# Two heads in one state product: an attention scan ahead of two feed-forward nets on one core

## The chip, the cores and the metric

The kernel runs on one core of a Trainium2 chip. The time is the device time of one execution in microseconds (us). Three executions of the kernel before took 524.62, 525.79 and 525.80 us; their median, 525.79 us, is the time before. One execution was recorded by the hardware profiler, and all rows below come from it.

The engines have short names: PE is TensorE (PEld its weight loads), DVE is VectorE, ACT is ScalarE, POOL is GpSimd, SP is the engine that issues transfers. Each runs its own instructions in order and waits on the others by semaphores. PSUM is the memory into which PE writes its sums; SBUF is the memory that all other operands live in.

## The reference, cut to what matters

Four batches of 768 rows, 8 heads, head size 32 (D), state size 16 (N). A chunked linear attention makes x, and two feed-forward nets follow, the second without a nonlinearity:

```python
for c in range(nc):                      # chunks of 32 in the reference
    L = exp(cum_i - cum_j) * causal
    y = (C B^T * L) x  +  (C state) * exp(cum)
    state = decay_full * state + sum_j B_j x_j * decay_from_j
x = y.reshape(3072, 256)
h = x @ w_in                             # 256 -> 2048
x = where(h > 0, h, exp(min(h, 0)) - 1) @ w_out
h = (x @ w1) * (x @ w2) @ w3             # 1024 wide
out = h @ w_out2                         # 256
```

## The kernel before, in words

**Tiling.** Time runs in 24 chunks of 128 columns (`k`; each is two sub-blocks `s` of 64), four to a tile of 512 columns (`t`, six tiles). A tile of `x` has its 256 features on 2 times 128 partitions. Every operand of the large products is kept as a high and a low float32r word (`mm3`, L381 to 384: three products of 128x128 by 128x512 for one exact one). A cast on ACT makes the high word, a subtraction (`take_lo`, L161) the low one.

**The scan.** `unit_u` (L658) makes, for two chunks, C times B (`cb_products`, L511) and the new part of the states (`u_products`, L548). A state tile has 128 rows: four groups of 32, each two heads of 16 states; its 64 columns are the 32 values of either head. So half of a group's block, the rows of one head under the values of the other, holds numbers that belong to no head. `decayed` (L526) and `states` (L559) follow on DVE. `unit_y` (L670) runs `y_products` (L582): for each chunk 16 products of x with the decayed C times B (L590), and then, for each chunk, sub-block, head of the pair (`g`) and group (`q`), one product of the 32 by 32 columns of that head with C (L598); C is laid out with zeros for the other head's 16 rows (`cd`, L530, made on POOL). `turned` (L544) moves the groups of odd chunks by one, so that group `q` of an even and of an odd chunk stand on different rows. `made_x` (L683) casts the result to xT and subtracts.

**The first net.** `unit_a` (L706) makes h of 256 features for one tile: 12 products of 512 columns; then `elu` (L713): exp and relu on ACT, a maximum on DVE (L722), the high word on ACT (L727), the low word on DVE (L729). `unit_b` (L737) multiplies by w_out: again 12 products. `half_a` (L701) makes only the first 256 columns of tile 0 for feature block `n`, into `early_h`; `unit_a` then makes the other half, if that `half_a` has run already.

**Weights.** They arrive as 64-bit words; each piece (L192) is shifted (`k`, DVE), scaled (`j`, ACT), joined (`K`, DVE), cast (`H`, ACT) and its low word taken (`I`).

**The second net** (`by_product`, `last_product`) runs from about 344 us on, on sums of its operands (one level of a seven-product scheme); its low words (`,`) and its sums (`}`, `>`, `{`) are on DVE, the operand sums (`*`) and half of the gates (`<`) on POOL.

**What sets the order.** The string `ORDER` (L37): each letter runs the next waiting step of its kind, and `in_order` (L646) fixes that each engine runs its instructions in the order in which the letters issue them. Nothing else plans. A step that waits holds back all that stands behind it on its engine.

Of the kernel before, what the change touches and what calls it, by code (L numbers as in the profile page):

```python
# [14 lines left out]
Q = 128  # L15
SUB = 2
# [21 lines left out]
094AAlU7AlC5Al5UCJCD566l8jCNk5K8JkHND6IjDQjND6KkHNkKQzzYNYzIvzjYNYjkaKjk!HaKXjkxIkNjKarkKMjsHMxKbIrNKxsXrLaHkBjLN8j8vsxX  # L38
BHKuWkPIrbDHMKjkIMKbWINsRXaWHLCNjLBbxCDrCttBjNsCakhVkiyxIrKbXkzsWzMHYYuhKNIaHiXIDbxDNrttjsyVaKzXzkHYYhNVaIxijMrkKbMsHxPL
raINhLjsaxijNhRbxXrLCCiaMSBSBrsBCbshxirLahKBiaxksHrIkbjsxCNKrKuHksbhItDVahtDjijykxirbMKHsMzbzhYPiNYuhKbXHtDtDjkyLaBzIzYY  # L40
INiaxKrXLHbHIsxNkhIRa1jBrMiaCxNCsrKwXxshkNribfsjCXjKHuFhMIatjDHNLIakxCDSiSr1bKxtLNrwsjskykfHFKhIaMzzHKjINibBkMBxYKYbhNri
PsuhbXjDtiXwtkDLykfhFRaHXHIziBNbxIYjLrwzBsNYKukHMfIbjFDMKtHNaDILXCkwxBLCNhtrKajsfjKhiaxiHrkIbFKHxINsrbhskyhSwPjzzYYMKiaH
XSIijMfBakxCFNHCrIaXxsrRwxsrsbfjKkFLahBiuLxbrtBDCHDItbshiKyhHbzXIzYi1CuhYMaDDXttwixMrLBafNLsbBxCFrCkNjsyhazijYkbKxzKr3Y%
&su&h=bitbhtD&D=y=S&Saz=YNziaxYrsaNh3xibxkrrbsshiahjijKbxkK%&ra&s^=hb=&ix&=ar=Nsax1rh3aNxirksb3jxKs@jakK%&=a@#&h3rib&s@&
=x=b=h#Nri^ahs^xia@N#rk#jxsbrKsaSkjSKh%b@i&=xb^h&@=#ahi&ribx#s3r1xsb&=h3^@iar=hbix/srsbh/i|ch_bmi/|#b_/G|e]_gncS[Em({|G}
)]_e>gn<c[*Em(.{G})],<e.>En,g.{*c[,(m)S}*g.1>e.,*G[<3nc,.d*](,mE.}G.{d.,<e],)ng>E,.c{[*dm,(G*.}d.<e]*,d$.d,$),ng>.d+*.(,
[dc,$E}.d@{em,<@d#nG#d*3]g@+)[#^(>E}*c@{e.<dn^dm+d@#G.,)]#*g$>E@(.#^[c{3.d}*m),.e.,G<ng>](,@^E[}c,dm,e.#g.,Gd,*]d{E+n*).
<d.{d[*,(>d)+*c}d+m<e.,2gn>3G[+(]c.}dm,E.3,d.,G.,d,*g{e<dn*)+.(]+2*d.}E.>[d{.c,<2em,).Gn*>g],d.,d.,c[E,md,*({G}*.d<]).e*
>$d,.g*n,c[d.+($,2dm,E.}G.,d]{e$,<)@+gn#d[*(>@E}.*c{e<dn#d.,^)m+d@.g#^@G>.d,@*d+@d#](^.,E[c{*dm}).#G<.>e@#dng]#c[,Em,({G
}g],).,e,*En>d[d+*.d{c<*dm,).+(.*G>.g}.d],<[e+En+2c.,dm{(d}d,G,e]<)$,g.+*dn>2[d,c*.+(.d}*.d,2mE,G*.e{d,n<).,d.>g](,[c,E}  # L50
m*d{e*dnG.)],(.>*d$}E.<g.,d.{[c,<$d+me$,2).g,d+[d>nG.d.d.+c],(mE}d,e{G,nd+]),g<(>.d$[d.Ed{}),<d>,d..,d,dd+++++
"""
HALF = 4
VECTOR_LO = 16
PIECES = [(("w_in", "w_out")[k == "o"], "iioiooiiiiooiooo"[:n].count(k)) for n, k in enumerate("iioiooiiiiooiooo")] + [("wo2", m) for m in range(4)] + [("w3", m) for m in range(16)] + [
# [36 lines left out]
XCOLS = (("x", DM), ("bn", NH * N), ("bt", 2 * R), ("cz", 2 * 2 * R), ("cp", SUB * 2 * R))  # L92
# [3 lines left out]
def kernel(  # L96
# [42 lines left out]
    side = const.tile([P, 2], F32, name="side")  # L139
    sel = act.tile([P, 2, 2, TT], F32R, tag="g", name="sel")[:SUB * CPT, 0, 0].rearrange("p (k s i) -> p k s i", k=CPT, s=SUB)  # L140
    begun = const.tile([P, CPT * SUB, R], F32, tag="begun", name="begun")

    def constants():

        V.memset(side, 0.0)
        A.activation(side, side, AF.Exp)

        G.memset(eye2, 1.0)
        G.affine_select(out=eye2, in_=eye2, compare_op=ALU.is_equal, fill=0.0, base=0,
                        pattern=[[-R, SUB], [-1, R]], channel_multiplier=1)  # L150
        n = SUB * CPT
        A.copy(sel, eye2[:n, 0, :n].rearrange("p (k s o) -> p k s o", k=CPT, o=1).to_broadcast([n, CPT, SUB, R]))
        V.tensor_tensor(out=eye2[:, 0], in0=eye2[:, 0], in1=eye2[:, 1], op=ALU.add)
        V.tensor_copy(eye, eye2[:, 0:1].to_broadcast([P, NH, R]))
        G.memset(begun, 0.0)

# [35 lines left out]
    class Piece:  # L192


        def __init__(self, name, src, room, dst):
            self.name, self.src, self.room, self.dst = name, src, room, dst
            self.lo, self.word, self.parts, self.half = G, None, None, 0

# [232 lines left out]
    def at_load(k):  # L431
        c = ck[k]
        all_ = att.tile([P, XC], F32, tag="xbc", name=f"xbc{k}", bufs=4)
# [9 lines left out]
        c["cp"] = cols_["cp"].rearrange("p (s f) -> p s f", s=SUB)  # L443
# [99 lines left out]

    def turned(k, p):  # L544

        return (p + k % 2) % 4

    def u_products(k, u):  # L548


        c = ck[k]
        for p in range(4):
            for s in halves(k):
                rows = slice(R * s, R * s + R)
                to = turned(k, p)
                T.matmul(u[32 * to:32 * to + 32, s], c["bd"][rows, 2 * p:2 * p + 2].rearrange("p h n -> p (h n)"),
                         c["x"][rows, 64 * p:64 * p + 64], start=True, stop=True, skip_group_check=True)

    def states(k, u):  # L559
# [4 lines left out]
        for s in halves(k):  # L564
            V.scalar_tensor_tensor(out=new[:, s], in0=state[k, s], scalar=pr_of(k)[:, s, R - 1:R], in1=u[:, s],
                                   op0=ALU.mult, op1=ALU.add)
            state[(k, 1) if s == 0 else (k + CPT, 0)] = new[:, s]

    def first_states(k, u):
# [3 lines left out]
        state[k, 1], state[k + CPT, 0] = new[:, 0], new[:, 1]  # L573
        later("8", next_state, k)

    def next_state(k):

        kept = att.tile([P, 2 * D], F32, tag="kept", name=f"kept{k}", bufs=1)
        G.tensor_tensor(out=kept, in0=state[k, 1], in1=ck[k]["pr"][:, 1, R - 1:R].to_broadcast([P, 2 * D]), op=ALU.mult)
        G.tensor_tensor(out=state[k + CPT, 0], in0=state[k + CPT, 0], in1=kept, op=ALU.add)  # L580

    def y_products(*chunks):  # L582
        for k, both in chunks:
            c = ck[k]
            for g in range(2):
                for s in range(SUB):
                    rows = slice(R * s, R * s + R)
                    for q in range(4):
                        h = 2 * q + g
                        T.matmul(both[32 * q:32 * q + 32, s, g], c["x"][rows, D * h:D * h + D], c["L"][rows, h],  # L590
                                 start=g == 0, stop=(k, s) not in state, skip_group_check=True)
        for g in range(2):
            for s in range(SUB):
                for k, both in chunks:
                    for q in range(4) if (k, s) in state else ():
                        at = turned(k, q)
                        rows = slice(32 * at, 32 * at + 32)
                        T.matmul(both[32 * q:32 * q + 32, s, g], state[k, s][rows, D * g:D * g + D], ck[k]["cd"][rows, s, g],  # L598
                                 start=False, stop=True, skip_group_check=True)

    def x_room(k):
        t, s0 = k // CPT, (k % CPT) * Q
        if k % CPT == 0:
            xT[t] = [act.tile([P, 2, TT], F32R, tag=f"xx{p}", name=f"xT{p}{t}", bufs=3) for p in ("h", "l")]
        return [v[:, :, s0:s0 + Q].rearrange("p g (s i) -> p s g i", s=SUB) for v in xT[t]]

    def by_head(y):
        return y.rearrange("p s (g i) -> p s g i", g=2)

    def parts_of(room):  # L610

        cb, u, both = (room[:, :, a:b] for a, b in ((0, 4 * R), (4 * R, 4 * R + 2 * D), (4 * R + 2 * D, 6 * R + 2 * D)))
        return cb, u, by_head(both)
# [3 lines left out]
    def first_room_of(k):  # L617
# [3 lines left out]
                first_rooms[2 + half][:, :, R * (k % 2):R * (k % 2) + R],  # L621
                first_rooms[2 + k % 2][:, :, 2 * R * (1 + half):2 * R * (2 + half)])

    def first_cb(*ks):
        for k in ks:
            cb, u, y = first_room_of(k)
            ck[k]["room"] = u, by_head(y)
# [3 lines left out]
    def first_u(*ks):  # L631
        for k in ks:
            u_products(k, ck[k]["room"][0])
        for k in ks:
            later("6", first_states, k, ck[k]["room"][0])

    def first_y(*ks):
        y_products(*((k, ck[k]["room"][1]) for k in ks))
        for k in ks:
            later("z", made_x, k, ck[k]["room"][1], A)  # L640
# [29 lines left out]
    def unit_y(k):  # L670

        two = [(j, by_head(banks(f"y{j}")[:, :, :2 * R])) for j in (k, k + 1)]
        y_products(*two)
        for j, both in two:
            later("z", made_x, j, both, A if j < 2 * CPT else V)
# [7 lines left out]
    def made_x(k, both, hi_eng):  # L683
        hi, lo = x_room(k)
# [28 lines left out]
    def elu(t, n, h):  # L713
# [9 lines left out]
        if not plain:  # L723
# [4 lines left out]
            yield "i"  # L728
            take_lo(V, lo, e, hi)  # L729
# [279 lines left out]
    for n, p in enumerate(queue):  # L1009
        p.lo = V if 0 < n < VECTOR_LO else G  # L1010

# [97 lines left out]
```

## Time and profile before

| | us |
|---|---|
| three executions | 524.62, 525.79, 525.80 |
| the profiled execution, its own time | 524.71 |
| its span, first to last instruction | 523.0 |
| PE busy | 508.8 (97%) |
| DVE, ACT, POOL busy | 428.8 (82%), 323.6 (62%), 204.4 (39%) |
| moved | 52.66 MB in 28177 packets |

A row of grouped instructions reads: line, engine, operation, output from inputs, shape, count, then busy time and mean duration in ns of one, then the idle time of the engine ahead of them and what ended it. A recorded matmul lasts longer than its share of PE's time, since matmuls overlap: the distance from start to start is the cost. A float32 product has two records, a float32r product one.

### The profile page before, as it was taken

The numbers are of one execution on the slowest core, as the hardware profiler recorded it, in microseconds if no ns is written. First come the engines' busy times: TensorE is split into PE (matmuls) and PEld (weight loads), VectorE is DVE, ScalarE is ACT, GpSimd is POOL, SyncE is SP. The second block draws the span as 40 slices with busy tenths as digits, with TensorE's granted clock in tenths as the row PEclk, the third lists the DMA queues.
The fourth block names the chain that finished last, engine by engine and source line by source line (L and its number), as shares of the span: only waits on it lengthen the run. The fifth ranks groups of instructions, "written<-read, shape, count | busy, mean of one in ns | idle before, by whom it ended". The sixth has DMA issues, their size and how long they took to land.

```text
span 523.0 us, 10654 instructions
## 1 busy us (share of the span) xinstructions
PE 508.8 (97%) x4330; PEld 411.2 (79%) x4330; DVE 428.8 (82%) x589; ACT 323.6 (62%) x482; POOL 204.4 (39%) x184
## 2 busy tenths in 40 slices
PE   5799999999999999999999999999989999999996
PEld 3675788778888888878788888888777888888885
DVE  6888989879897996867766797869999989988845
ACT  2585587655754385535476787747766577765650
POOL 3223004205430544122203333967477465755401
PEclk9999999999999999999999999999999999999999
DMA  8993473147555635053202321001000110001002
GB/s 297 348 277 132 134 207 126 41 143 235 170 158 150 222 108 174 1 160 104 69 35 77 106 80 47 35 0 61 0 22 21 61 41 20 1 20 41 21 1 80
DMA packets 28177, 52.66 MB, mean 101 GB/s; under 512 B 2304, under 2 KB 10880, under 8 KB 28128
## 3 DMA queue, kind: packets, MB, share of 16 engines
q1 hardware_dynamic: 27984, 51.85, 30.4%
q8 instruction: 34, 0.56, 0.4%
q14 instruction: 15, 0.12, 0.1%
q10 hardware_dynamic: 144, 0.13, 0.1%
HBM read 45.58 MB, written 6.39 MB: 99 GB/s over the span
## 4 chain that ended last, share of the span: by engine, by line
PE 91%; DVE 6%; issue 1%; DMA 0%; ACT 0%; DVEq 0%
PE acc L382 9%; PE acc L384 9%; PE h L382 9%; PE acc L383 9%; PE h L383 9%; PE h L384 9%; PE p L382 4%; PE p L384 3%; PE p L383 3%; PE acc L745 3%; PE p_d L382 2%; PE p_d L384 2%; PE p_d L383 2%; PE p_E L382 2%; PE p_E L383 2%; PE p_E L384 2%
## 5 line engine op out<-in xcount | busy, mean ns | idle before, releaser
L715 ACT ACTIVATE e<-h 128x1024 f32<-128x1024 f32 x48 | 49.2, 1025 | 58.0 <-PE h L384 55.5
L382 PE MATMUL h<-xTh,w_in 128*128 128x512 f32 (+1 forms) x200 | 80.0, 400 | 0.8 <-ACT xTh L685 0.8
L383 PE MATMUL h<-xTl,w_in 128*128 128x512 f32 (+1 forms) x200 | 77.7, 389 | 0.0
L384 PE MATMUL h<-xTh,w_in 128*128 128x512 f32 (+1 forms) x200 | 77.5, 388 | 0.0
L162 DVE TENSOR_TENSOR g<-e,g 128x1024 fp32r<-128x1024 f32 x44 | 60.1, 1370 | 15.5 <-ACT g L727 15.4
L382 PE MATMUL acc<-g,w_out 128*128 128x512 f32 x176 | 69.6, 396 | 0.0
L722 DVE SCALAR_TENSOR_TENSOR e<-e,h 128x1024 f32<-128x1024 f32 x44 | 53.3, 1214 | 19.7 <-ACT e L717 19.6
L384 PE MATMUL acc<-g,w_out 128*128 128x512 f32 x176 | 68.6, 390 | 0.0
L383 PE MATMUL acc<-g,w_out 128*128 128x512 f32 x176 | 68.5, 389 | 0.0
L727 ACT CAST g<-e 128x1024 fp32r<-128x1024 f32 x44 | 46.2, 1049 | 30.0 <-PE acc L384 26.5
L717 ACT ACTIVATE e<-e 128x1024 f32<-128x1024 f32 x48 | 50.7, 1059 | 0.8
L382 PEld LDWEIGHTS h<-xTh,w_in 128*128 128x128 f32 x200 | 38.6, 193 | 9.4 <-issue 1.8
L383 PEld LDWEIGHTS h<-xTl,w_in 128*128 128x128 f32 x200 | 38.5, 193 | 7.8 <-issue 0.7
L384 PEld LDWEIGHTS h<-xTh,w_in 128*128 128x128 f32 x200 | 38.6, 193 | 7.6
L162 POOL TENSOR_TENSOR w<-raw_wc,w 128x512 fp32r<-128x512 f32 x16 | 23.9, 1502 | 51.5 <-ACT w L236 48.6
L536 POOL TENSOR_TENSOR xbc<-xbc,pr 128x256 f32<-128x256 f32 (+1 forms) x24 | 22.9, 965 | 50.9 <-DMA L<-a_cut 30.7
L382 PEld LDWEIGHTS acc<-g,w_out 128*128 128x128 f32 x176 | 33.0, 188 | 7.4
L384 PEld LDWEIGHTS acc<-g,w_out 128*128 128x128 f32 x176 | 33.0, 188 | 7.0
L383 PEld LDWEIGHTS acc<-g,w_out 128*128 128x128 f32 x176 | 33.1, 188 | 6.6
L504 POOL TENSOR_TENSOR xbc<-xbc,L 128x128 f32<-128x128 f32 x24 | 15.1, 634 | 58.1 <-DVE L L498 37.7
L899 POOL TENSOR_TENSOR room_l<-room_l,room_o 128x512 f32<-128x512 f32 x12 | 19.8, 1647 | 32.8 <-DVE room_o L896 19.1
L498 DVE TENSOR_TENSOR_SCAN L<-L,eye 128x512 f32<-128x512 f32 x20 | 27.3, 1368 | 2.0 <-DMA L<-a_cut 2.0
(427 smaller groups left out, 1278.2 us busy)
## 6 DMA issues: line engine op xcount, KB each, us to landing
xbc<-in_xc SPq DMA_DIRECT2D x24, 512.0 KB, 6.3
raw_wc<-in_w3t SPq DMA_DIRECT2D x16, 512.0 KB, 4.3
L<-a_cut SPq DMA_DIRECT2D x40, 128.0 KB, 4.8
raw_wi<-in_w_in SPq DMA_DIRECT2D x8, 512.0 KB, 8.6
raw_wo<-in_w_out SPq DMA_DIRECT2D x8, 512.0 KB, 6.4
x_dram<-x SPq DMA_DIRECT2D x6, 512.0 KB, 4.9
room_s<-x_dram SPq DMA_DIRECT2D x12, 256.0 KB, 4.3
out_t<-out SPq DMA_DIRECT2D x11, 256.0 KB, 2.0
```

The costliest lines, as they stand in the source:

```text
L162: eng.tensor_tensor(out=lo, in0=raw, in1=hi.bitcast(F32), op=ALU.subtract)
L382: T.matmul(out, wlo, xhi, start=first, stop=False, **kw)
L383: T.matmul(out, whi, xlo, start=False, stop=False, **kw)
L384: T.matmul(out, whi, xhi, start=False, stop=last, **kw)
L498: V.tensor_tensor_scan(out=flat, data0=wide, data1=eye.rearrange("p h s -> p (h s)"), initial=0.0, op0=ALU.mult, op1=ALU.add)
L536: G.tensor_tensor(out=c["cd"][:, n:], in0=c["cd"][:, n:], in1=c["pr"].rearrange("p s (o i) -> p s o i", o=1)[:, n:].to_broadcast([P, SUB - ...
L715: A.activation(e, h, AF.Exp)
L717: A.activation(e, e, AF.Relu, scale=-1.0, bias=1.0)
L722: V.scalar_tensor_tensor(out=gt[t, n] if plain else e, in0=e, scalar=-1.0, in1=h, op0=ALU.mult, op1=ALU.max)
L727: A.copy(hi, e)
L745: T.matmul(acc, word_of(n)[:, j, es], g[:, j], start=m == 0, stop=False)
L899: GATE[m % 2].tensor_tensor(out=s["two"], in0=s["two"], in1=s["u2"], op=ALU.mult)
```

## The change

State tiles are set to zero outside each head's own block, on POOL, by one multiplication with a mask (`own_heads`, letter `?`), 24 times. C is kept without its zeros, so `cd` multiplies half as many elements, and a chunk's transfer has 448 KB in place of 512 KB. One product takes 32 rows by all 64 columns of a group and so serves two heads. Outputs now go by four heads and two chunks to a PSUM tile, instead of by one chunk. `turned` is gone.

Beside it: 13 of the 44 low words of the elu (`T`) are taken on POOL; 21 of 44 weight shifts run on ACT; xT casts of chunks 8 to 15 run on ACT. The order of the first weight pieces is another (five of w_in first), and the whole `ORDER` string is another. In the string of before the second `v` (`half_a` of block 1) stands behind the third `a` that follows `a` of block 1; in the new one ahead of `a` of block 1. The new string starts with all four `A`, and moves DVE's `7` behind three scans (`l`).

```diff
-094AAlU7AlC5Al5UCJCD566l8jCNk5K8JkHND6IjDQjND6KkHNkKQzzYNYzIvzjYNYjk
+094AAlAl5Al5U7UJD6lk?C6j?!DNCkKC5jD5QHN8JKzIzY66NYHk?jD8kNK?jCI8QkNvK8zzY
...
+SCALAR_Z = 4
+POOL_LO = "001000100101000000010100101100001101000110000000"
+SCALAR_LOW = "11011000000110010000100011111001011110011100"
...
+        G.memset(head, 1.0)
...
+        V.tensor_reduce(out=own, in_=head.rearrange("p (b g) -> p g b", g=2), op=ALU.add, axis=AX.X)
...
         def shifted(self):
-            V.tensor_scalar(self.low, self.low, 29, None, op0=ALU.logical_shift_right)
+            if self.scalar_low:
+                A.activation(self.low, self.low, AF.Copy, scale=15 / 16 * 2.0 ** -29 * (1 - 2.0 ** -8))
+            else:
+                V.tensor_scalar(self.low, self.low, 29, None, op0=ALU.logical_shift_right)
...
-        c["cd"] = c["cp"].rearrange("p s (w i) -> p s w i", w=2)
-        G.tensor_tensor(out=c["cd"][:, n:], in0=c["cd"][:, n:],
-                        in1=c["pr"].rearrange("p s (o i) -> p s o i", o=1)[:, n:].to_broadcast([P, SUB - n, 2, R]),
-                        op=ALU.mult)
+        c["cd"] = c["cp"]
+        G.tensor_tensor(out=c["cd"][:, n:], in0=c["cd"][:, n:], in1=c["pr"][:, n:], op=ALU.mult)
...
+        later("?", own_heads, new[:, :len(halves(k))])
+
+    def own_heads(new):
+        n = new.shape[1]
+        G.tensor_tensor(out=new.rearrange("p s (g d) -> p s g d", g=2), in0=new.rearrange("p s (g d) -> p s g d", g=2),
+                        in1=own.rearrange("p (o g e) -> p o g e", o=1, e=1).to_broadcast([P, n, 2, D]), op=ALU.mult)
...
+        for s in range(SUB):
+            for n, k in enumerate(chunks):
+                for q in range(4) if (k, s) in state else ():
+                    rows = slice(32 * q, 32 * q + 32)
+                    T.matmul(rooms[q // 2][64 * (q % 2):64 * (q % 2) + 64, s, n], state[k, s][rows], ck[k]["cd"][rows, s],
+                             start=False, stop=True, skip_group_check=True)
...
+            later("z", made_x, k, f, rooms[f], A if k < SCALAR_Z * CPT else V)
...
-            yield "i"
-            take_lo(V, lo, e, hi)
+            pool = POOL_LO[t * NA + n] == "1"
+            yield "T" if pool else "i"
+            take_lo(G if pool else V, lo, e, hi)
```

## Rows read from the trace of the kernel before

**Rows 1.** Page, part 1: busy time (share of the span) and instructions.

```profile
PE 508.8 (97%) x4330; PEld 411.2 (79%) x4330; DVE 428.8 (82%) x589; ACT 323.6 (62%) x482; POOL 204.4 (39%) x184
```

**Rows 2.** Windows: stretch, its length, then busy PE, PEld, DVE, ACT, POOL, granted clock, DMA.

```profile
20.71:353.00 332.29, 332.29 (x3287) 269.69 (x3288) 266.89 (x367) 212.82 (x277) 107.65 (x107) 1.00 0.39 123
...
364.00:368.00 4.00, 3.55 (x15) 2.55 (x14) 4.00 (x6) 1.40 (x3) 1.78 (x2) 1.00 0.00 0
380.00:386.00 6.00, 4.63 (x21) 3.51 (x20) 6.00 (x7) 2.94 (x5) 5.29 (x5) 1.00 0.14 45
386.00:516.00 130.00, 129.98 (x571) 106.80 (x571) 112.35 (x156) 80.24 (x148) 67.41 (x44) 1.00 0.07 23
```

**Rows 3.** Waits of PE: who waited for whom, us in total, times, longest.

```profile
PE p L382 <- DVE room_l L902: 1.8, 2, 1.4
```

**Rows 4.** Chain that ended last, one `y` and one `u`: start, us, what.

```profile
57.02 0.79 PE y L598 x53
...
61.39 0.38 PE s L556 x30
```

**Rows 5.** Groups by line and shape: the state products of the ten `y` units.

```profile
L598 PE MATMUL y<-xbc,st 32*32 32x64 f32 x640 | 8.6, 222 | 0.0
```

**Rows 6.** Timeline of PE, state products of chunks 2 (f) and 3 (acc_f): start, us.

```profile
19.20 0.33 PE L598 MATMUL f<-xbc,st 32*32 32x64 f32 x4
19.23 0.33 PE L598 MATMUL acc_f<-xbc,st 32*32 32x64 f32 x4
19.31 0.33 PE L598 MATMUL f<-xbc,st 32*32 32x64 f32 x4
```

**Rows 7.** Timeline of PE about the second `half_a`: start, us.

```profile
37.30 0.39 PE L384 MATMUL h<-xTh,w_in 128*128 128x512 f32 x1
37.53 0.28 PE L382 MATMUL h<-xTh,w_in 128*128 128x256 f32 x1
37.65 0.28 PE L383 MATMUL h<-xTl,w_in 128*128 128x256 f32 x1
```

**Rows 8.** Groups by line and shape: products of 256 columns (one of three lines).

```profile
L384 PE MATMUL h<-xTh,w_in 128*128 128x256 f32 x12 | 4.2, 352 | 0.0
```

**Rows 9.** Timeline of the start, DVE, POOL, ACT and PE: start, us.

```profile
6.78 1.22 DVE L498 TENSOR_TENSOR_SCAN L<-f,eye 128x512 f32<-128x512 f32 x1 [1.74 <-PE f L487]
...
9.17 1.20 DVE L498 TENSOR_TENSOR_SCAN L<-f,eye 128x512 f32<-128x512 f32 x1
...
13.13 0.45 POOL L536 TENSOR_TENSOR xbc<-xbc,pr 128x128 f32<-128x128 f32 x1
...
13.98 0.71 DVE L224 SCALAR_TENSOR_TENSOR raw_wi<-raw_wi 128x512 uint32<-128x512 uint32 x1
...
14.72 0.68 ACT L236 CAST w_in<-raw_wi 128x512 fp32r<-128x512 f32 x1 [1.59 <-DVE raw_wi L224]
...
15.04 1.87 DVE L528 TENSOR_TENSOR L<-f,L 128x512 f32<-128x512 f32 x3
...
15.48 1.31 POOL L162 TENSOR_TENSOR w_in<-raw_wi,w_in 128x512 fp32r<-128x512 f32 x1 [0.18 <-ACT w_in L236]
...
20.33 0.42 DVE L162 TENSOR_TENSOR xTl<-f,xTh 128x256 fp32r<-128x256 f32 x1 [1.54 <-ACT xTh L685]
...
20.71 0.55 PE L382 MATMUL h<-xTh,w_in 128*128 128x256 f32 x1 [0.83 <-ACT xTh L685]
```

**Rows 10.** Timeline of PE where its pace changes: start, us.

```profile
24.93 0.41 PE L382 MATMUL h<-xTh,w_in 128*128 128x256 f32 x1
25.14 0.41 PE L383 MATMUL h<-xTl,w_in 128*128 128x256 f32 x1
```

**Rows 11.** Groups by line and shape: operations that change engine, and the new one's nearest.

```profile
L162 POOL TENSOR_TENSOR w<-raw_wc,w 128x512 fp32r<-128x512 f32 x16 | 23.9, 1502 | 51.5 <-ACT w L236 48.6 <-DMA L<-a_cut 2.7
...
L504 POOL TENSOR_TENSOR xbc<-xbc,L 128x128 f32<-128x128 f32 x24 | 15.1, 634 | 58.1 <-DVE L L498 37.7 <-DMA raw_wo<-in_w_out 17.5 <-issue 2.9
...
L565 DVE SCALAR_TENSOR_TENSOR st<-st,pr,s 128x64 f32<-128x64 f32 x36 | 9.6, 276 | 2.6 <-PE s L556 2.0
```

More of the change, by code (lines that the diff above doesn't have):

```diff
@@ L42 @@
[L42 to L46, printed above, removed]
@@ L139 @@
     side = const.tile([P, 2], F32, name="side")
+    head, own = const.tile([P, NH], F32, name="head"), const.tile([P, 2], F32, name="own")
     sel = act.tile([P, 2, 2, TT], F32R, tag="g", name="sel")[:SUB * CPT, 0, 0].rearrange("p (k s i) -> p k s i", k=CPT, s=SUB)
@@ L573, in first_states @@
         state[k, 1], state[k + CPT, 0] = new[:, 0], new[:, 1]
+        later("?", own_heads, new)
         later("8", next_state, k)
@@ L578, in next_state, with y_products @@
         kept = att.tile([P, 2 * D], F32, tag="kept", name=f"kept{k}", bufs=1)
-        G.tensor_tensor(out=kept, in0=state[k, 1], in1=ck[k]["pr"][:, 1, R - 1:R].to_broadcast([P, 2 * D]), op=ALU.mult)
+        G.tensor_tensor(out=kept, in0=state[k, 1], in1=pr_of(k)[:, 1, R - 1:R].to_broadcast([P, 2 * D]), op=ALU.mult)
         G.tensor_tensor(out=state[k + CPT, 0], in0=state[k + CPT, 0], in1=kept, op=ALU.add)
-    def y_products(*chunks):
-        for k, both in chunks:
+    def y_products(chunks, rooms):
+        for n, k in enumerate(chunks):
             c = ck[k]
-            for g in range(2):
+            for f, room in enumerate(rooms):
                 for s in range(SUB):
@@ L588, in y_products, with x_room, by_chunk @@
                     for q in range(4):
[L589 to L601, printed above, removed]
+                        h = 4 * f + q
+                        T.matmul(room[32 * q:32 * q + 32, s, n], c["x"][rows, D * h:D * h + D], c["L"][rows, h],
+                                 start=n == 0, stop=(k, s) not in state, skip_group_check=True)
+        for s in range(SUB):
+            for n, k in enumerate(chunks):
+                for q in range(4) if (k, s) in state else ():
+                    rows = slice(32 * q, 32 * q + 32)
+                    T.matmul(rooms[q // 2][64 * (q % 2):64 * (q % 2) + 64, s, n], state[k, s][rows], ck[k]["cd"][rows, s],
+                             start=False, stop=True, skip_group_check=True)
+    def x_room(k, f):
         t, s0 = k // CPT, (k % CPT) * Q
-        if k % CPT == 0:
+        if t not in xT:
             xT[t] = [act.tile([P, 2, TT], F32R, tag=f"xx{p}", name=f"xT{p}{t}", bufs=3) for p in ("h", "l")]
-        return [v[:, :, s0:s0 + Q].rearrange("p g (s i) -> p s g i", s=SUB) for v in xT[t]]
-    def by_head(y):
-        return y.rearrange("p s (g i) -> p s g i", g=2)
+        return [v[:, f, s0:s0 + 2 * Q].rearrange("p (j s i) -> p s j i", j=2, s=SUB) for v in xT[t]]
+    def by_chunk(y):
+        return y.rearrange("p s (j i) -> p s j i", j=2)
     def parts_of(room):
-        cb, u, both = (room[:, :, a:b] for a, b in ((0, 4 * R), (4 * R, 4 * R + 2 * D), (4 * R + 2 * D, 6 * R + 2 * D)))
-        return cb, u, by_head(both)
+        return room[:, :, :4 * R], room[:, :, 4 * R:4 * R + 2 * D]
     first_rooms = []
@@ L632, in first_u @@
         for k in ks:
[L633 removed]
+            u_products(k, ck[k]["room"])
         for k in ks:
[L635 removed]
+            later("6", first_states, k, ck[k]["room"])
     def first_y(*ks):
[L638 removed]
+        at = 2 * R * (1 + ks[0] // 2)
+        rooms = [by_chunk(room[:, :, at:at + 2 * R]) for room in first_rooms[2:]]
+        y_products(ks, rooms)
+        for f in range(2):
+            later("z", made_x, ks[0], f, rooms[f], A)
         for k in ks:
[L640 removed]
             later("M", at_l, CPT + k)
@@ L670, in unit_y @@
     def unit_y(k):
[L672 to L675, printed above, removed]
+        rooms = [by_chunk(banks(f"y{k}_{f}")[:, :, :2 * R]) for f in range(2)]
+        y_products((k, k + 1), rooms)
+        for f in range(2):
+            later("z", made_x, k, f, rooms[f], A if k < SCALAR_Z * CPT else V)
         if k % CPT == 0 and k // CPT + 1 < NTILE:
```

65 lines of the change are left out of this document (32 added, 33 removed).

## The prediction

> **What bounds the kernel now.** I read the page's busy shares first: PE is busy for 508.8 of 523.0 us [rows 1]. Such a share is a mean over stages, so the windows come next. From 20.71 to 353 us PE is never idle; it is idle for 0.45 us in 364 to 368 and for 1.37 us in 380 to 386, and from 386 to 516 us again for almost nothing [rows 2]. The list of PE's waits names what ends those two holes: the gate's additions on DVE (L902), which is busy for every microsecond of both stretches [rows 2, 3]. So there are three places where time can go. Before 20.71 us a chain through DVE, POOL, ACT and PE sets the end. From there to 353 us PE's own work sets it, and only what shortens PE's list counts. In 353 to 386 us DVE's list counts a little. Work taken off DVE between 20.71 and 353 us is worth nothing by itself: DVE is idle there for 332.3 - 266.9 = 65 us, while PE waits for nobody.
>
> **State products.** A `y` unit spends 0.79 us on them [rows 4]; it has 64 records, two for each of 32 products, and there are ten such units [rows 5]. The new unit has 16 products, 32 records. Whether this halves the time depends on how many run side by side. A product of 32 rows by 32 columns takes one place in the array. At the start, four records of one chunk and four of the next start within 0.03 us, and the next four follow 0.11 us after the first ones [rows 6]: eight at a time, on the eight places that `turned` provides, each place taken for 0.107 us (at the slower pace of that moment; below). At the pace of the steady part, twice as fast, a place is taken for some 0.053 us, so eight at a time would pass 64 records in 0.43 us; the unit's 0.79 contains some waiting beyond that. The new products take 32 rows (q) by 64 columns (half q mod 2): four distinct places, the same four for both chunks and both sub-blocks. So I expect four at a time: 32 records in 8 x 0.053 = 0.43 us, plus what a group costs beside its places. The `u` products show that: 32 records on eight places take 0.38 us [rows 4], 0.17 more than 4 x 0.053. Together 0.60 us, 0.19 less than now, ten times: **-1.9 us**. The bounds: if eight still go side by side, 0.38 us as for `u`, ten times 0.41 = -4.1; if a product with twice the columns costs twice, nothing. At the start the four chunks gain nothing by the same count: half the records at half the number of places.
>
> The trace has 0.79 / 32 = 25 ns for a product in `y` and 0.38 / 16 = 24 ns in `u` [rows 4]. The Trainium skill, "TensorE: Matmul & The Clock Gate", section "Wait — 56ns, not 53.3ns?", states a floor of about 25 ns from start to start however small the product is; the trace agrees with that number. By that rule alone the unit would fall to 16 x 25 ns = 0.40 us and the change would bring 3.9 us here in place of 1.9.
>
> **A half that was made twice.** In the order of before the second `half_a` stands behind the full `a` of block 1, so its 12 products of 256 columns are made again and never read. They stand in the trace from 37.53 us, 0.12 us from start to start, behind products of 512 columns at 0.23 [rows 7], and there are 12 for each of the three lines, four more than one used `half_a` and its other half need [rows 8]. In the new order `half_a` stands ahead, and `a` of block 1 makes only the other half: 12 products of 512 columns become 12 of 256, 12 x (0.23 - 0.12) = **-1.3 us**, and PE waits for nothing there that could take it back.
>
> **The start.** The first product of the net starts at 20.71 us, released by the casts of x [rows 9]. Before, DVE runs scan, decay (the 1.2 us between the first scan's end at 8.00 and 9.17), two scans, `decayed`, the fourth scan, then weight shifts and joins, and three `decayed` from 15.04 us at 0.62 each [rows 9]; the second of the four ends near 15.7. New order on DVE: three scans from 6.78 us at 1.21, decay 1.2, `decayed` 0.62 to 0.69, scan 1.21, `decayed`: 6.78 + 3.6 + 1.2 + 0.7 + 1.2 + 0.7 = 14.2. So `y` of chunks 0 and 1 can end about 1.5 us earlier. `y` of 2 and 3 then needs, on DVE, two joins (0.71 each), `decayed`, two subtractions (0.42), a shift (about 0.5) and the last `decayed`: 14.2 + 4.1 = 18.3. On POOL it needs the masks of 2 and 3, which stand behind the first low word: join ends at 14.9, cast 0.68, low word 1.31, so 16.9; then mask, the pair of small state operations (0.65), mask, `cd` (0.45), a mask at 0.4 to 0.63: near 18.8. The state products follow, and `half_a`, whose x and weights are ready by 17.1, starts near 19.4: -1.3. That is uncertain by 1.2 either way, and part may be lost: up to 25.14 us products of 256 columns start 0.21 us apart [rows 10], the pace of the lower level, 1.2 GHz (the granted clock's column shows 1.00 throughout); later 0.12, the pace of 2.4 GHz. If that moment stays where it is while work starts earlier, half of the gain goes. I take **-1.0**, bounds -2.5 and +0.5. The chunk's smaller transfer is hidden: PE is still at the products of the cut a when chunks 2 and 3 arrive.
>
> **Masks and `cd` on POOL.** The nearest row is POOL's 128x128 product, 0.63 us [rows 11]: 24 masks add 15.1 us, `cd` at half size gives back about 0.4 each, and 13 low words of the elu, twice the 1.50 us of a 128x512 subtraction [rows 11], add 39. POOL rises from 204 to about 250 us, under half of the span. The mask is a new wait: behind it stand the state products, and behind those all of PE. From a `u` to its `y` lie at least two units of the net, 2 x 12 x 0.23 = 5.5 us. The chain is two `decayed` and four `states` (0.28 each [rows 11]), 2.4 us on DVE, then two masks, 1.3: 3.7 us. It fits where POOL is free; behind a 3.0 us low word it doesn't quite. I allow **+0.2** (bounds 0 and +6).
>
> **The rest.** Shifts and casts on ACT lie beside PE's unbroken list and cost nothing as long as ACT (62%) follows; uncovered, one late cast would cost PE its 0.7 us. In 364 to 386 us the new order puts four low words ahead of the fourth column's gate where the old one put eight, but the products `d` that want them come at the same place; of the 1.82 us idle I expect **-0.4** (bounds -1.8 and +2.5).
>
> **Sum.** -1.9 - 1.3 - 1.0 + 0.2 - 0.4 = -4.4, from the profiled execution's own 524.71: 520.3 us. That execution lies 1.08 us under the median, and two of three runs stand at 525.8, so the new median can lie up to 1.1 above its profile: I name 520.6.
>
> **Rivals.** (a) The state products fall to the `u` pace: 2.2 us more go, 518.4. For it: the 24 to 25 ns in both rows, the rule above. Against: only four places. (b) Neither the start nor the state products move, only the double half goes: 523.4 from the profile, 523.9 as a median. For it: new steps on POOL at the start, and a chain there with many short links. (c) The second stage gets worse: DVE is full in 353 to 386 us, and a subtraction a microsecond late stops PE; with +3 there, 523.6. (d) Slower: the mask comes too late. Place: `u` and `y` of chunks 10 and 11, two units apart, with a low word of 128x1024, one of 128x512 and a `cd` ahead of the masks in POOL's order: 3.0 + 1.5 + 0.6. If POOL begins those only when `u` ends, PE waits 3.7 + 5.1 - 5.5 = 3.3 us; chunks 6 and 7 are as close. It decides from some 0.6 us a unit, 6 us in all: two such waits and some small ones, 527. For it: POOL's durations swell beside DVE. Against: POOL is idle for over half of the span and itself mostly waits for DVE.
>
> **How the numbers follow.** Chances: the forecast 50%, (a) 22%, (b) 15%, (c) 7%, (d) 6%. A difference under 0.3% (1.6 us) can't be told from none; the line is 524.2. The forecast, (a), half of (b) and half of (c) fall under it: 84%; the rest of (b), most of (c)'s rest and a little of (d) are within: 10%; slower 6%. The range, 516.8 to 524.2, reaches down to (a) with a start that gains 2.5 us and up to (b).
>
> **What would show it.** State products of a `y` unit in the chain at about 0.60 us (0.38: rival a; 0.79: b). 128x256 products x16 a line, h of 512 columns 12 fewer in all. First product of the net near 19.4 us, and where the pace changes. No wait of PE on POOL in 20 to 350 us; a list with masks in it shows (d). PE's idle time in 350 to 390 us against 1.82. The forecast is wrong if PE's list of waits has a row over 1 us between 20 and 350 us, or if the net starts after 20.7 us.

## The result, and the profile after

The changed kernel takes 519.82 us (median of four executions, 518.89 to 520.39) where the kernel before takes 525.79; the ratio is 0.9881 [0.9862, 0.9900]. The forecast was 520.6. The profiled execution took 519.32 us (span 517.6) against 524.71 (span 523.0): 5.39 us less.

I cut both traces at two places: where the first 24 products of the net, 256 columns wide, are done (the end of the start), and where the second net's first product begins. The times of the cuts are start times of records; "end" is the last product of PE.

| | before | after | difference |
|---|---|---|---|
| first product of the net | 20.71 | 21.32 | +0.61 |
| start, up to the 25th product of the net | 25.88 | 25.64 | -0.24 |
| from there to the second net | 311.17 | 308.27 | -2.90 |
| second net | 181.48 | 179.22 | -2.26 |

The second net's first product stands at 337.04 us before (not near 344) and at 333.92 us after. The first product of the first net comes 0.61 us later in the profile after, and the start is still shorter. Its 24 products take 4.32 us in place of 5.17, because they go over from 0.21 to 0.12 us a product earlier: at 24.45 us after, at 25.52 us before (the last section comes back to this).

The total is right within 0.8 us, but the terms are not: the start, forecast at -1.0, gives almost nothing here, and the second net, forecast at -0.4, gives 2.3. First the page's parts 1 and 5 of the kernel after (engines' busy time; then POOL's new low words):

```profile
PE 504.3 (97%) x3978; PEld 408.4 (79%) x3978; DVE 406.6 (79%) x548; ACT 338.1 (65%) x511; POOL 242.0 (47%) x224
...
L171 POOL TENSOR_TENSOR g<-e,g 128x1024 fp32r<-128x1024 f32 x13 | 32.6, 2506 | 41.5 <-ACT g L738 34.9
```

Against [rows 1], DVE gave up 22.2 us and POOL took on 37.6, near the 250 us forecast. A low word on POOL takes 2.51 us, where I had put 3.0. PE lost 4.5 us of its own work. The chain of waits after, at one `y` unit (start, us, what; L609 is the line of the state products, L603 that of the products of x with L):

```profile
51.62 0.79 PE y L603 x53
52.41 0.62 PE y L609 x32
```

Where 64 records took 0.79 us [rows 4], 32 take 0.62. Between one unit's first state product and the next work on PE lie 0.785 us before and 0.623 after, in all ten units alike (two of before had 0.82 and 0.84). The groups by line and shape after:

```profile
L395 PE MATMUL h<-xTh,w_in 128*128 128x256 f32 x16 | 5.5, 342 | 0.0
...
L609 PE MATMUL y<-xbc,st 32*64 32x64 f32 x320 | 6.9, 223 | 0.0
```

640 records became 320 [rows 5], and x12 became x16 [rows 8]: `half_a` is used now. All of PE's waits after, by total (us, times, longest):

```profile
PE f L500 <- ACT a_hl L439: 4.5, 1, 4.5
PE f L609 <- POOL xbc L549: 1.2, 1, 1.2
PE f L603 <- ACT st L584: 1.1, 1, 1.1
PE f L603 <- issue: 0.8, 1, 0.8
PE f L603 <- DVE xTl L171: 0.8, 1, 0.8
PE h L395 <- DVE g L733: 0.4, 1, 0.4
PE f L534 <- DMA xbc<-in_xc: 0.2, 1, 0.2
```

All but the row of 0.4 us lie before 21 us. The wait on POOL's `cd` (L549) runs from 19.69 to 20.90 us. No row names the masks (L578), so rival (d) did not occur; the gate's rows [rows 3] are gone, and rival (c), a longer second net, did not occur either; and there is one new wait, 0.4 us at 42 us on the maximum of an elu (L733). The windows show the second net (stretch, length, busy PE, PEld, DVE, ACT, POOL, granted clock, DMA):

```profile
364.00:368.00 4.00, 4.00 (x19) 3.34 (x18) 2.93 (x5) 2.39 (x5) 3.83 (x3) 1.00 0.00 0
380.00:386.00 6.00, 6.00 (x29) 4.95 (x28) 6.00 (x8) 4.73 (x9) 5.28 (x5) 1.00 0.00 0
386.00:512.00 126.00, 125.93 (x553) 103.37 (x552) 108.59 (x151) 76.07 (x141) 63.23 (x42) 1.00 0.07 24
```

PE has no hole in either stretch, where it had 0.45 and 1.37 us [rows 2]. The second net starts 3.1 us earlier here, so these stretches hold not quite the same work, but the list of waits above has no row in the second net at all. Where the start went is seen on POOL and PE, in the chain of waits after (start, us, what; L578 mask, L592 and L593 the small state operations, L549 `cd`):

```profile
16.40 1.25 POOL w_in L171
17.65 0.54 POOL st L578
18.20 0.26 POOL kept L592
18.46 0.07 issue
18.53 0.79 POOL st L593
19.32 0.81 POOL st L578
20.12 0.73 POOL xbc L549
20.86 0.04 issue
20.90 0.37 PE f L609 x2
...
21.39 0.51 PE h L395
```

I had POOL's last `cd` of the start done near 18.8 us; it is done at 20.85. The low word ahead ends 0.75 us later than I had it: its cast is done at 15.32, but another small pair (L592, L593) stands ahead of it in POOL's order and holds POOL until 16.4. From there the mask, the small pair, the mask and `cd` take 3.2 us (17.65 to 20.85) where I allowed 1.9. In POOL's timeline a mask took 0.40 us and a `cd` 0.32 at 12.4 to 13.1 us, but 0.85 and 0.76 at 19.3 to 20.8; what makes them longer there is not shown.

### The profile page after: what moved, and what is told of

The parts are those of the page before. It is cut to its first block, busy times and chain, and to the rows that moved or that the text cites. A ratio compares the mean times of both kernels' runs of the same rounds, so it can differ in the third digit from the quotient of the medians.

```text
span 517.6 us, 9978 instructions
## 1 busy us (share of the span) xinstructions
PE 504.3 (97%) x3978; PEld 408.4 (79%) x3978; DVE 406.6 (79%) x548; ACT 338.1 (65%) x511; POOL 242.0 (47%) x224
## 4 chain that ended last, share of the span: by engine, by line
PE 95%; POOL 2%; DMA 1%; DVE 1%; SPq 0%; issue 0%; DVEq 0%; ACT 0%; POOLq 0%
PE acc L395 10%; PE acc L396 9%; PE acc L397 9%; PE h L395 9%; PE h L396 9%; PE h L397 9%; PE p L395 4%; PE p L397 4%; PE p L396 4%; PE acc L757 3%; PE p_E L395 2%; PE p_E L397 2%; PE p_E L396 2%; PE p_d L397 2%; PE p_d L396 2%; PE p_d L395 2%
## 5 line engine op out<-in xcount | busy, mean ns | idle before, releaser
L733 DVE SCALAR_TENSOR_TENSOR e<-e,h 128x1024 f32<-128x1024 f32 x44 | 53.4, 1214 | 37.3 <-ACT e L728 33.3
L395 PE MATMUL h<-xTh,w_in 128*128 128x512 f32 (+1 forms) x200 | 78.8, 394 | 0.4 <-DVE g L733 0.4
L397 PE MATMUL h<-xTh,w_in 128*128 128x512 f32 (+1 forms) x200 | 76.7, 383 | 0.0
L171 DVE TENSOR_TENSOR g<-e,g 128x1024 fp32r<-128x1024 f32 x31 | 42.1, 1357 | 15.0 <-ACT g L738 14.9
L171 POOL TENSOR_TENSOR g<-e,g 128x1024 fp32r<-128x1024 f32 x13 | 32.6, 2506 | 41.5 <-ACT g L738 34.9
L171 POOL TENSOR_TENSOR w<-raw_wc,w 128x512 fp32r<-128x512 f32 x16 | 22.5, 1410 | 25.6 <-ACT w L249 12.3
L511 DVE TENSOR_TENSOR_SCAN L<-L,eye 128x512 f32<-128x512 f32 x20 | 25.8, 1298 | 0.1
```

What stands on the lines that cost most here:

```text
L171: eng.tensor_tensor(out=lo, in0=raw, in1=hi.bitcast(F32), op=ALU.subtract)
L395: T.matmul(out, wlo, xhi, start=first, stop=False, **kw)
L397: T.matmul(out, whi, xhi, start=False, stop=last, **kw)
L511: V.tensor_tensor_scan(out=flat, data0=wide, data1=eye.rearrange("p h s -> p (h s)"), initial=0.0, op0=ALU.mult, op1=ALU.add)
L733: V.scalar_tensor_tensor(out=gt[t, n] if plain else e, in0=e, scalar=-1.0, in1=h, op0=ALU.mult, op1=ALU.max)
```

## The experiments

The theories. State products: a product holds one of four places in the array (mine), against a fixed pace for each record or column. Second net: its own new order, against the work taken off DVE. Start: POOL's order, against something ahead of it.

**The half ahead, alone.** The kernel before, with one letter moved. (In the old string that letter stands behind the second `a` that follows `a` of block 1, not behind the third.)

```diff
-...kaKjk!HaKXjk...LN8j8vsxX
+...kaKjk!HvaKXjk...LN8j8sxX
```

> The kernel before with one letter moved: the half of block 1 is made ahead of that block's products, as in the changed kernel, so that it is used and not made twice. Theory (PE's list is the bound there, the half was waste): 128x256 products go from 12 to 16 a line, h of 512 columns lose 4 a line, and the end comes 1.3 us earlier (1.1 to 1.5), near 523.4 against a profile of 524.7. Rival (DVE or the arrival of weights sets the pace of the first 60 us, and PE's list has slack): PE waits where the work is gone, time unchanged within 0.3 us.

525.24 us, ratio to before 0.9975 [0.9953, 0.9997], about -1.3 us. In the trace the middle is 1.63 us shorter (309.54 against 311.17), 1.37 of it from start to start in the products of h; the rest is spread over other products. The groups have x16, and the `y` units are as before. The second net stays at 181.47. The term of -1.3 stands, as -1.3 by times (the interval reaches from -0.2 to -2.5) and up to -1.6 by this trace. Its profile's start is 2.6 us longer, which an order changed only from the second `a` on can't explain; this comes back below.

**The products alone.** The new code with the order of before (a `?` behind each `t` and `6`), with no offloads:

```diff
-SCALAR_Z = 4
-POOL_LO = "001000100101000000010100101100001101000110000000"
-SCALAR_LOW = "11011000000110010000100011111001011110011100"
+SCALAR_Z = 2
+POOL_LO = "0" * 48
+SCALAR_LOW = "0" * 44
...
-PIECES = [(("w_in", "w_out")[k == "o"], "iiiiiooioioooioo"[:n].count(k)) ...
+PIECES = [(("w_in", "w_out")[k == "o"], "iioiooiiiiooiooo"[:n].count(k)) ...
```

> The kernel before with the new state products, masks and unpadded C alone: the old order of all steps (a mask right behind the step that makes the state), low words, shifts and casts on their old engines, the half still made twice. Theory (the products give 0.165 us in each of ten units and the mask hides on POOL): 1.7 us faster than before, near 523.0, the start within 0.7 us of 20.7, PE's holes of 1.8 us still there. Rival (without the new order the mask's wait shows on PE): a wait of PE on the masks in each unit, time at or above that of before.

524.22 us, 0.9958 [0.9941, 0.9975]. The unit takes 0.623 us, the middle falls by 1.74, 0.08 of it in the two longer units of before, the second net stays (181.42), and no wait of PE names a mask, although here the masks stand right behind the states. One number missed: the net starts at 21.70 us, 1.0 behind 20.7 where 0.7 was allowed (the table below has why). So the products bring 1.7 us in either order, and with the half 1.7 + 1.6 - 0.4 (the new wait) = 2.9: that is the middle's whole difference.

**Eight places.** The changed kernel with the groups of odd chunks moved by one row group again, and each chunk's state products writing its own bank. Each product then reads the state and C of one sub-block twice in place of both sub-blocks, so part of the state's share of y is left out; the number and shape of the products is the same.

```diff
+    def turned(k, p):
+        return (p + k % 2) % 4
...
+                to = turned(k, p)
+                T.matmul(u[32 * to:32 * to + 32, s], ...
...
-        for s in range(SUB):
+        for again in range(2 if chunks[0] >= CPT else 1):
...
+                s = n if k >= CPT else 1
+                for q in range(4):
+                    rows = slice(32 * turned(k, q), 32 * turned(k, q) + 32)
+                    T.matmul(rooms[q // 2][64 * (q % 2):64 * (q % 2) + 64, n, n], state[k, s][rows], ...
```

> The changed kernel with the state products of the ten y units on eight places of the array in place of four: the same 16 products of 32 rows by 64 columns a unit, but odd chunks stand one group of rows further, and each unit makes one sub-block of each chunk twice and leaves out the other, so part of the state's share of y is left out. Theory (a unit is held by its four places, each taken for 0.053 us by a record): state products of a unit fall from 0.62 us to about 0.40, the end comes 2.2 us earlier, near 517. Rival (64 columns of weights, or a fixed pace of 39 ns a product, hold it): 0.62 us stays, time unchanged within 0.3 us.

517.01 us in one execution, with the middle 2.13 us shorter than in the changed kernel. The same unit in its chain of waits:

```profile
51.26 0.79 PE y L608 x53
52.05 0.42 PE y L615 x32
```

The same 32 records take 0.42 us on eight places and 0.62 on four. Their starts show why. The first group of state products in PE's timeline, before, after and on eight places:

```profile
56.95 0.28 PE L598 MATMUL y<-xbc,st 32*32 32x64 f32 x8
52.34 0.28 PE L609 MATMUL y<-xbc,st 32*64 32x64 f32 x4
51.98 0.31 PE L615 MATMUL y<-xbc,st 32*64 32x64 f32 x8
```

In the changed kernel four records start within 0.02 us, and from the second group on the next four follow 0.058 us behind; on eight places it is eight within 0.05 us, and again 0.058 us to the next eight. The places are what held them; a fixed pace per record, or a price by columns, would have left 0.62. The run on eight places also writes four banks at a time in place of two, but the kernel before starts eight records at a time on two banks, so the banks are not the reason. The Trainium skill, "TensorE: Matmul & The Clock Gate", section "Wait — 56ns, not 53.3ns?", puts a floor of about 25 ns from start to start. The trace does not show that floor here: single records start 7 ns apart, and on eight places 16 products start within 0.27 us, 17 ns a product. The mean over the unit, 0.416 / 16 = 26 ns, comes near it only because the last 0.15 us, in which no product starts, is in it. A kernel of this form that does all of the work wasn't tried.

**The old order of the second net.** The changed kernel, with the order of before from the first `c` on (less one `#`, which the new order has issued by then):

```diff
-i/|m_b/GSg]e|[EncS{(1m_)|}G>3e]_g.<cn,*[(mE}G.{e],<)nE>g*{.c[,dm*(...
+mi/|b_/G|e]_gncS[Em({|G})]_e>gn<c[*Em(.{G})],<e.>En,g.{*c[,(m)S}*g...
```

> The changed kernel, but from the first product of the second net on every engine follows the order of the kernel before; all else as in the changed kernel. Theory (the two holes of PE at 364 to 386 us went because that stage's own order was changed): PE's holes of about 1.8 us come back, time near 521.1 against a profile of 519.3. Rival (they went because DVE carries 22 us less work ahead of that stage and enters it earlier): no hole comes back, time unchanged within 0.4 us.

522.03 us, 0.9915 [0.9898, 0.9932]. The second net takes 181.49 us, as before, and its holes are back. PE's wait in it:

```profile
PE p L395 <- DVE room_l L914: 1.9, 2, 1.4
```

and a window (columns as above):

```profile
380.00:390.00 10.00, 8.60 (x38) 6.83 (x37) 9.40 (x13) 6.31 (x12) 7.16 (x6) 1.00 0.04 14
```

All offloads are still there, so the relief of DVE did not close the holes; the stage's order did.

**Offloads undone.** The changed kernel with all `T` turned into `i`, all weight shifts but four of the first five, and the xT casts of chunks 8 to 15 on DVE:

```diff
-SCALAR_Z = 4
-POOL_LO = "001000100101000000010100101100001101000110000000"
-SCALAR_LOW = "11011000000110010000100011111001011110011100"
+SCALAR_Z = 2
+POOL_LO = "0" * 48
+SCALAR_LOW = "11011" + "0" * 39
```

> The changed kernel with the work moved off DVE put back on it, from the sixth weight piece on: all 44 low words of the elu, 39 weight shifts and the casts of chunks 8 to 15 are on DVE again, in the changed order. Theory (work off DVE is worth nothing while PE's list is the bound): time unchanged within 0.5 us, DVE some 25 us busier, no new wait of PE between 60 and 350 us. Rival (the lighter DVE is what lets the new order run without holes): waits of PE on DVE appear or the holes of 1.8 us come back, slower by 1.5 us or more.

520.54 us, 0.9885 [0.9869, 0.9901]: the changed kernel's ratio. Its second net takes 179.28, so the new order runs there without its holes on the fuller DVE. DVE is busy for 417.8 us, 11 more than in the changed kernel, where I expected some 25. The middle is 1.4 us longer. Two waits of PE named "issue", which no other run has behind 28 us and which I had not expected, make up 1.3 of that: one in L609 at 108 us (0.4 us idle, 0.7 from start to start), one in L534 at 153 us (0.3 and 0.6). That leaves 0.1 us for the work put back on DVE itself; whether it has a part in the two stops is not shown.

**The gates ahead of the low words.** The kernel before, with one `,` moved behind a `>`, and one `#` and one `+` behind the next:

```diff
-...d.,<e],)ng>E,.c{[...<d#nG#d*3]g@+)[#^(>E}*c@...
+...d.,<e])ng>,E,.c{[...<d#nG#d*3]g@)[^(>+#E}*c@...
```

> The kernel before with two gates moved ahead in DVE's list: the gate of column 3 ahead of one low word, the gate of column 5 ahead of one low word and one addition into the output; nothing else. Theory (PE's holes of 1.8 us are there because those gates stand behind other work on DVE, while PE waits for the bank that they read): at least 1.2 of the 1.8 us go, time 1.2 to 1.8 us under that of before, the stage of the second net 180.0 us or less in place of 181.5. Rival (DVE is full in that stretch, and work put behind the gates is missed a little later): the holes move to other products, stage length unchanged within 0.3 us.

524.94 us, 0.9979 [0.9955, 1.0003]. The times don't tell it from before by themselves; the trace does. The second net takes 179.95 us, 1.53 less. Both waits for the gate (L902) are gone, and another of 0.7 us has come, for the sum (L896) that now stands behind the work moved back, as the rival had it in part:

```profile
PE p_E L382 <- DVE room_o L896: 0.7, 1, 0.7
```

Three letters give two thirds of what the whole new order of that stage gives. The holes came from gates that stood behind other work, two low words and an addition, on a full DVE.

**POOL's start.** The changed kernel with `cd` of chunk 3 (`C`) ahead, and two of the small state operations (`8`) behind the last mask:

```diff
-...jD5QHN8JKzIzY66NYHk?jD8kNK?jCI8QkNvK8...
+...jD5QHNCJKzIzY66NYHk?jDkNK?j88I8QkNvK8...
```

> The changed kernel with three steps of POOL's list at the start in another order: cd of chunk 3 goes ahead of the first low word, and the two small state operations of chunks 0 and 1, each a pair, behind the masks of chunks 2 and 3. Theory (POOL's late cd held the second y at 20.90 us): PE's wait on POOL there (1.2 us) goes, the net's first product starts near 20.0 in place of 21.3, and the end comes 0.7 to 1.3 us earlier, less what the wait for code takes back (0.8 us in the changed kernel's profile, 0.6 to 2.6 in the others). Rival (the wait for code or DVE is the bound there): the first product stays at 21 or later, time unchanged within 0.4 us.

518.46 us (517.94 to 519.67), 0.9848 [0.9828, 0.9868]: the fastest of those that do all of the work, 1.4 us under the changed kernel's median. PE's waits behind 14 us, up to the net, no longer name POOL:

```profile
PE f L603 <- DVE L L541: 0.7, 1, 0.7
PE f L603 <- DVE xTl L171: 0.4, 1, 0.4
PE f L603 <- issue: 0.3, 1, 0.3
```

The net begins at 19.40 us, the time that I had forecast for the changed kernel. `cd` and the small operations were moved together, so which of them counts is not shown.

**The code's packet.** In every trace but one PE stands still near 17 us behind its 444th or 445th recorded load or product, whatever the order of the kernel, and the wait is named "issue". Each time one packet of 16384 bytes on queue 8 (kind "instruction") has landed 1.28 to 1.46 us before PE goes on. In the remaining trace (the next run) PE comes to that place 1.7 us behind the packet and passes it without a stop. The trace before has 34 such packets and the one after has 31, one for every 255 and 257 recorded loads and products of PE (8660 and 7956). So I take them for PE's code; no run moved this packet at will, so that PE waits for it rests on these thirteen traces. I thought it late behind the weights' transfers, and held back weight loads on the version above:

```diff
-...66NYHk?...HKjvMIHk...
+...66MNYHk?...HKjvIHk...
```

> As the run with POOL's three steps in another order, and besides the load of the cut a of chunk 4 stands ahead of the loads of four weight pieces in SP's list, which holds these 2 MB back until the first y is done. Theory (PE's wait for code at the start is a 16384-byte packet that queues behind weight transfers): the packet lands before 15.5 us, PE's wait named issue falls under 0.3 us, the net's first product starts by 19.7. Rival (the packet is asked for late, and the other transfers have no part in it): it lands after 16 us as in the other runs, and the wait stays at 0.6 us or more.

518.87 us, 0.9855 [0.9838, 0.9872]: no gain, and the net begins at 20.41 where 19.7 was stated. The transfers fell from 384 to 201 GB/s in 15 to 18 us, and the packet landed at 16.07 all the same, between the 15.52 and 16.87 of two executions without this change. That the weights hold it up is not supported; one trace beside that scatter can't exclude it either.

**Three kernels once more**, unchanged, for their starts alone:

> The changed kernel once more, for its start alone. Two theories of where the net starts. The chain's: the first product comes when POOL's cd is done, so it stays within 0.3 us of 21.32, and PE's wait named issue within 0.3 of 0.81. The code packet's: PE resumes 1.3 to 1.7 us behind the landing of one packet of code, whose time differs from one execution to the next of the same program; then the packet lands over 0.5 us from 16.4, and PE's resuming moves with it, away from 17.86.

> The kernel before once more, for its start alone. The chain's theory: first product within 0.3 us of 20.71, issue wait within 0.3 of 0.60. The code packet's: the packet lands over 0.5 us from 16.25, PE resumes 1.3 to 1.7 us behind it, and the first product moves too where the packet is later (up to 23, as in the run of the half alone).

> The order with cd ahead of two masks once more. The chain's theory: first product within 0.3 us of 19.40. The code packet's: its 19.40 came with the earliest packet of all runs (landed at 15.52); a later one moves the first product to 20.4 to 21.7.

519.89, 527.16 and 518.91 us, one execution each. The start of all runs, in us; "packet" is its landing, "PE on" the start of the record behind PE's stop (for "loads held back", of the record at the same place):

| run | packet | PE on | first product | from PE on | end of start |
|---|---|---|---|---|---|
| before | 16.25 | 17.71 | 20.71 | 3.00 | 25.88 |
| before, again | 18.34 | 19.75 | 22.74 | 2.99 | 28.24 |
| half ahead | 18.56 | 20.01 | 23.01 | 3.00 | 28.50 |
| gates ahead | 18.30 | 19.75 | 22.75 | 3.00 | 27.72 |
| products alone | 18.21 | 19.49 | 21.70 | 2.21 | 27.24 |
| after | 16.42 | 17.86 | 21.32 | 3.46 | 25.64 |
| after, again | 15.64 | 17.04 | 20.81 | 3.77 | 25.79 |
| old second net | 16.95 | 18.38 | 20.84 | 2.46 | 26.07 |
| offloads undone | 16.91 | 18.30 | 20.71 | 2.41 | 25.45 |
| eight places | 17.48 | 18.89 | 20.74 | 1.85 | 25.29 |
| POOL's start | 15.52 | 16.84 | 19.40 | 2.56 | 23.84 |
| POOL's start, again | 16.87 | 18.15 | 20.35 | 2.20 | 24.79 |
| loads held back | 16.07 | 17.79 | 20.41 | 2.62 | 24.69 |

The same program before starts its net at 20.71 in one execution and at 22.74 in the next. Its chains of waits (start, us, what), first in the profile before:

```profile
17.12 0.60 issue
```

and in the second execution:

```profile
17.29 2.46 issue
19.75 0.31 PE f L598
```

The stop is 1.86 us longer, all work from PE's going on to the first product takes the same 3.0 us, and the rest of the net agrees within 0.12 us (311.29 and 181.47). So the 524.71 of the profile before, and its 20.71, were an execution with an early packet; the 28 timed executions of that kernel in this study have a median of 526.2 us. The chain's theory missed all three first products; of its numbers only the wait of the changed kernel, 0.52 us for 0.81, came within the 0.3 allowed. The packet's held for the kernels before and after. For POOL's start once more the net began at 20.35, just under the 20.4 that was the least. There a wait on DVE's low word ends at 17.69, 0.82 us behind the packet, and the stop follows it; it is short enough to show only among the weight loads, and ends 1.29 us behind the packet:

```profile
18.15 0.18 PEld L603 LDWEIGHTS f<-L,xbc 64*32 64x32 f32 x6 [0.27 <-issue]
```

## Why the prediction came out right

**State products.** Forecast -1.9, measured -1.7 (ten times 0.785 - 0.623, and two longer units). The 0.60 us came out at 0.62, and for the reason given: four at a time, a group every 0.058 us where I had 0.053, and 0.42 on eight places. Rival (a) rested on the 25 ns of both rows, which are a mean over a whole unit; it needed places that this change gave up with `turned`. Rival (b), in which the products do not move, fell with the same runs. What I passed over is the old unit. By the count of places its eight groups of eight need as long as the new unit's eight groups of four, and the change would bring next to nothing, as I said of the start. Its first 32 records do start in groups of eight, within 0.27 us; the other 32 start nearly one by one and take 0.37, in eight of the ten units alike and longer in two. This slower half, the "some waiting beyond that" of the prediction, is 0.11 of the 0.16 us gained a unit. What slows it is not shown.

**The half.** Forecast -1.3; alone it gives -1.3 by times, -1.6 by its trace.

**Masks and `cd`.** Forecast +0.2 for a wait on POOL after the start; no such wait came in any run behind the start. What came, and I had not named it, is 0.4 us on an elu's maximum at 42 us, in all runs with the new order there and in none with the old. Which part of the order brings it wasn't tried.

**The second net.** This is the term I mis-sized: -0.4 against -2.26. The step that failed: "four low words ahead of the fourth column's gate where the old one put eight, but the products `d` that want them come at the same place". The count was off: up to that gate the old string has eight low words and the new one seven, and between the third gate and the fourth it is five and four. And the number of low words was not what counted. The gate (L902, a multiplication, not an addition) was what PE waited for, and it stood behind other work on a DVE that was busy for the whole stretch; moving three letters, two low words and an addition, removed 1.53 us, so what stood right ahead of the gate was the wait itself. My lower bound, -1.8, was the recorded idle time, and that is less than the holes cost. PE's timeline before, at the two holes:

```profile
366.36 0.40 PE L384 MATMUL p<-room_i,s 128*128 128x512 f32 x1
367.21 0.50 PE L382 MATMUL p<-room_i,s 128*128 128x512 f32 x1 [0.45 <-DVE room_l L902]
...
383.49 0.39 PE L384 MATMUL p<-room_i,s 128*128 128x512 f32 x1
385.25 0.50 PE L382 MATMUL p<-room_i,s 128*128 128x512 f32 x1 [1.37 <-DVE room_l L902]
```

From start to start it is 0.85 and 1.76 us in place of 0.23, and the product behind each follows after 0.34: 2.4 us in all, where the idle time is 1.82, since a record lasts longer than its share.

**The start.** Forecast -1.0, measured -0.24 between two profiles, with the first product at 21.3 where I had 19.4. The step that failed is POOL's list, which I timed at 18.8 us and which ended at 20.85: the low word ahead of the first mask ended later, and the five short operations behind it took 3.2 us where the rows had let me put 1.9. That POOL's order put `cd` too late is shown: with `cd` ahead and the small pairs behind, the net begins at 19.40. From PE's going on it then takes 2.56 us in place of 3.77 where the packet lands near 15.6, and 2.20 in place of 2.41 and 2.46 where it lands near 16.9: 1.2 us with an early packet, 0.2 to 0.3 with a later one. What I did not see is that both profiles' starts hang on a packet that moves by over 2 us between executions of one program. The order of before takes 3.0 us after it, whatever its time. The new one takes 1.85 to 2.46 where the packet is late, since POOL and DVE have gone on meanwhile; and more where it is early, since POOL then ends last. So the profile before has an early start of its kernel (three later ones of its order came 2 us later), and the difference of two profiles undersells the change. By medians the start gives 519.82 - 525.79 + 2.90 + 2.26 = -0.8 us, and -1.2 against the 526.2 of the 28: near -1.0, for reasons that I had only half.

**The sum.** -1.7 - 1.6 + 0.4 - 2.3 - 0.2 = -5.4 between the profiles, against -4.4. The allowance of 0.3 us for an early profile pointed the right way. Both of my signs that the forecast is wrong came: the net did start after 20.7 us, and PE's list has a row over 1 us that reaches beyond 20 us, the 1.2 us on POOL's `cd` up to 20.90. The total still held because the second net gave back what the start kept; that is luck. (In the chances, the forecast, (a) and the two halves add up to 83%, not 84%.)

## What to carry to other kernels

When small products are merged, count the places in the array that they occupy before counting the products: half the products on half the places gave 21% (0.785 to 0.623), not 50%, and most of that because the old ones did not keep the pace of their own places. Where a profile shows an engine full and PE waiting for it, look at what stands ahead of the awaited instruction in that engine's order; moving it was worth nearly as much here, by the trace, as the products (1.5 and 1.7 us). And take the start of a kernel from several executions before you compare two.

## What the runs showed that I had not expected

In twelve of thirteen traces PE stands still near 17 us, for 0.3 to 2.6 us, and all thirteen fit a packet of code on queue 8 as the reason. Of the 2.45 us between the two profiled executions of the kernel before (524.71, 527.16), 2.36 lie in the start; whether the whole spread of that kernel, 523.5 to 527.7, is of this kind I have not shown. What sets the packet's time is open: with less traffic it did not come earlier.

The moment at which products of 256 columns go from 0.21 to 0.12 us from start to start moved as well, by 1.0 us between two executions of the changed kernel (24.45 and 25.44), and the earlier one belongs to the execution whose net began later:

```profile
24.04 0.41 PE L395 MATMUL h<-xTh,w_in 128*128 128x256 f32 x1
24.26 0.36 PE L396 MATMUL h<-xTl,w_in 128*128 128x256 f32 x1
24.45 0.28 PE L397 MATMUL h<-xTh,w_in 128*128 128x256 f32 x1
24.57 0.28 PE L395 MATMUL h<-xTh,w_in 128*128 128x256 f32 x1
```

These are PE's records in the profile after; before, the two at 0.21 us stand as late as 25.14 [rows 10]. The second execution of the changed kernel shows the granted clock on both sides of that moment (columns as above, the clock is the third from the end):

```profile
12.00:15.00 3.00, 1.77 (x112) 1.29 (x112) 3.00 (x5) 2.73 (x6) 2.96 (x8) 1.00 1.06 395
15.20:25.30 10.10, 7.09 (x101) 6.14 (x102) 8.85 (x17) 7.23 (x17) 6.24 (x11) 0.50 1.06 302
25.50:30.00 4.50, 4.50 (x34) 4.28 (x34) 2.81 (x5) 3.22 (x4) 0.00 (x0) 1.00 1.05 249
```

So 0.21 us is the pace at 0.50, 1.2 GHz, and 0.12 the pace at 1.00, 2.4 GHz. In the other traces the clock has no record ahead of the change of pace, so the 1.00 that the column shows there, as in the prediction, tells nothing. My fear that this moment would stay where it is was not borne out, but what moves it I can't say.
